# The first chunk's MLP operand made transposed in PSUM, and its opening written out in program order

## The chip, the cores and the metric

The kernel runs on one core of a Trainium2 chip. The metric is the device time of one execution in microseconds. The kernel before took 1027.79, 1029.85 and 1028.12 us in three runs; the median is 1028.12 us.

## The reference

All data is float32. B = 8 batches, H = 8 heads, S = 576 positions, head size D = 64, so a token has 512 features.

```python
scores = where(mask[h], (q @ k.T) / sqrt(D), -1e9)   # heads 0-3: the last 32 positions
attn   = softmax(scores)                             # heads 4-7: every 4th of the last 128
x      = concat_heads(attn @ v)                      # (B, S, 512)
u      = x + ((x.T @ U) @ V).T                       # U: 576x32, V: 32x576, over positions
out    = u + relu(u @ w1) @ w2                       # w1: 512x2048, w2: 2048x512
```

## The kernel before, in words

**The MLP.** The 4608 tokens are 36 tiles of 128 rows. Three tiles make a chunk of 384 tokens; there are 12 chunks. In a chunk the 2048 hidden features are worked through in 16 slices of 128 (index f). `layer1(f)` (L822) is twelve matmuls of 128x384 on TensorE (PE): each float32 operand is split into a high and a low part, and the products high·high (`w1h`·`uth`), low·high (`w1l`·`uth`) and high·low (`w1h`·`utl`) are summed for four blocks of 128 features (index k). ScalarE (ACT) then makes `hh`, the relu rounded to the high part (L833), VectorE (DVE) makes the rest `hl` (L834), and `layer2(f)` (L838) is nine matmuls into three accumulators. On PE the order is layer1(0), layer1(1), layer2(0), layer1(2), layer2(1) and so on.

**The weights** arrive during chunk 0 as raw 64-bit words, two pieces for a slice (`w1` and `w2` of it), after three small pieces (0: `ut`, 1: `vt`, 2: `uv`). So piece 3+2f is the w1 of slice f and piece 4+2f its w2; a buffer `v_7` holds piece 7, the w1 of slice 2. A piece passes through `narrowed` (two ACT operations, L189 and L190), `add_low` (a shift on DVE, L194, and an add on DVE or GpSimd (POOL), L196) and `finish` (the high part by a cast, on ACT at L200 or on DVE at L202, then the low part by a subtract on POOL, L203). `weight_step` (L265) finishes piece i-3, adds piece i-2, narrows piece i-1 and sends for later pieces, and counts i up.

**The opening, batch 0's attention.** Nine groups of four units. For a group g: its k comes by DMA and is spread on POOL (`spread_q`, L306), `score` (L397) puts scores in PSUM, `soften` runs on DVE (L416) and ACT (the exponential, L420), `turn_pe` transposes on PE (L431), ACT copies the result to SBUF as `pt`, `product` multiplies by v on PE (L454), and `place` (a sum, a reciprocal and one or two multiplies on DVE, L460 to L484) writes x. Plain groups write rows of x directly; dilated groups write `xp`, whose rows are permuted, and DMAs (`x<-xp`) bring them to x's order. Then `t_first` (L520) multiplies by U, `t_evict` splits the result `ts`, `mix` (L556) multiplies by V and adds to x on DVE (L558), and `transp` transposes u on PE (L587) and splits it into `uth` (ACT, L592) and `utl` (DVE, L593), which layer1 of chunk 0 reads.

**Order.** `first_batch` (L637) is issued in program order on PE, DVE, ACT and SP; after it a scheduler orders the instructions by priority. Before the first slice five weight steps are issued, then four after each slice of chunk 0, with a late priority, so that the scheduler may place them. Work for batch 1 and later stands in `queue` at positions counted in chunks and is taken out at `slot()` (L816), which is called six times in a slice. PSUM is one pool: in the opening the scores use the accumulators' three buffers, the transposes the two of `ph`, and the products `pv` three of their own.

Of the kernel before, what the change touches and what calls it, by code (L numbers as in the profile page):

```python
# [138 lines left out]
def attention_moe_kernel(ctx: ExitStack, tc: tile.TileContext, qk0, qk1, qk2, vv, masks, wide, ident, ut, vt, uv, w1, w2, out):  # L139
# [88 lines left out]
    def finish_w(f, layer, n):  # L228
        def go(v):
# [3 lines left out]
            narrow_c(v, h, l, nc.vector if n % L_ON_DVE == 0 else nc.gpsimd, n % 4 < H_ON_ACT)  # L233
# [31 lines left out]
    def weight_step():  # L265
        i = at.get(0, NSMALL)
# [6 lines left out]
        if NSMALL <= i - 2 < NPIECE and i - 2 not in added:  # L273
            add_low(i - 2, nc.vector)
# [182 lines left out]
    def place(g, pv):  # L457
# [29 lines left out]
        for t, to, n, r in sorted(moves):  # L487
# [473 lines left out]
```

## Time and profile before

| | before |
|---|---|
| median of the runs | 1028.12 us |
| the profiled execution's own time | 1031.81 us |
| its span in the trace | 1029.3 us |
| mean granted PE clock | 0.978 |
| first matmul of layer1(0) | 53.17 us |
| last matmul of layer1(15) in chunk 0 starts | 167.07 us |
| first matmul of chunk 1 | 179.68 us |
| PE busy / DVE / ACT / POOL | 988.1 / 593.6 / 387.4 / 306.7 us |

The profile is of one execution. Its own time is 2.5 us above its span, which is what lies ahead of the first and behind the last instruction, and 3.7 us above the median of the runs. A row of the timeline has the start in us, the busy time in us, engine, line, operation, output<-inputs, shapes and a count of instructions drawn together; brackets tell the idle time ahead and what ended it. A row of the stage table has a stretch, its length, and for PE, weight loads, DVE, ACT and POOL the busy us (and the instructions), then the granted clock, the share of the DMA engines and GB/s. A row of a group has the count, the summed busy us, the mean ns, the idle time ahead and what ended it.

### The profile page before, as it was taken

The numbers are of one execution on the slowest core, as the hardware profiler recorded it, in microseconds if no ns is written. First come the engines' busy times: TensorE is split into PE (matmuls) and PEld (weight loads), VectorE is DVE, ScalarE is ACT, GpSimd is POOL, SyncE is SP. The second block draws the span as 40 slices with busy tenths as digits, with TensorE's granted clock in tenths as the row PEclk, the third lists the DMA queues.
The fourth block names the chain that finished last, engine by engine and source line by source line (L and its number), as shares of the span: only waits on it lengthen the run. The fifth ranks groups of instructions, "written<-read, shape, count | busy, mean of one in ns | idle before, by whom it ended". The sixth has DMA issues, their size and how long they took to land.

```text
span 1029.3 us, 17998 instructions
## 1 busy us (share of the span) xinstructions
PE 988.1 (96%) x5904; PEld 864.9 (84%) x5904; DVE 593.6 (58%) x1972; ACT 387.4 (38%) x946; POOL 306.7 (30%) x519
## 2 busy tenths in 40 slices
PE   7589986999999999999999999999999999999998
PEld 6378865988888888888898888988888888899997
DVE  3489667676446863766556773666646865311211
ACT  5477445344233441434323541434323442111110
POOL 3266315345022630425222540325313440000000
PEclk9879997899999999999999999999999999999999
DMA  9558445343223422333233422334223421400000
GB/s 248 168 185 283 139 126 153 84 125 103 74 68 96 136 77 72 115 100 110 66 85 96 131 82 70 110 105 113 84 69 100 127 56 31 117 1 1 31 1 31
DMA packets 96764, 102.06 MB, mean 99 GB/s; under 512 B 12801, under 2 KB 83393, under 8 KB 96673
## 3 DMA queue, kind: packets, MB, share of 16 engines
q1 hardware_dynamic: 96672, 100.93, 34.2%
q8 instruction: 47, 0.77, 0.3%
q14 instruction: 45, 0.36, 0.1%
HBM read 78.86 MB, written 17.30 MB: 93 GB/s over the span
## 4 chain that ended last, share of the span: by engine, by line
PE 85%; DVE 2%; DMA 1%; ACT 1%; issue 0%; POOL 0%; DVEq 0%; SPq 0%; ACTq 0%
PE acc L845 38%; PE ph L828 37%; PE pv L454 4%; PE s L384 3%; PE t L534 2%; PE m L556 1%; PE s L397 1%; DMA raw<-w 1%; DVE v L196 1%; DMA zd<-z 0%; DVE v L194 0%; DVE x L870 0%; ACT v L189 0%; DVE z L566 0%; DVE x L558 0%
## 5 line engine op out<-in xcount | busy, mean ns | idle before, releaser
L845 PE MATMUL acc<-w2h,hh 128*128 128x512 f32 x576 | 230.1, 401 | 6.9 <-ACT hh L833 6.9
L845 PE MATMUL acc<-w2l,hh 128*128 128x512 f32 x576 | 230.1, 400 | 0.0
L834 DVE SCALAR_TENSOR_TENSOR hl<-ph,hh 128x384 fp32r<-128x384 f32 x192 | 106.2, 553 | 189.9 <-ACT hh L833 189.2
L845 PE MATMUL acc<-w2h,hl 128*128 128x512 f32 x576 | 211.1, 398 | 1.4 <-DVE hl L834 1.4
L361 POOL TENSOR_TENSOR qks<-qkr,qks 128x160 fp32r<-128x160 f32 x192 | 103.0, 536 | 361.9 <-ACT qks L360 260.1
L833 ACT ACTIVATE hh<-ph 128x384 fp32r<-128x384 f32 x192 | 93.3, 486 | 268.7 <-PE ph L828 257.6
L828 PE MATMUL ph<-utl,w1h 128*128 128x384 f32 x768 | 176.6, 343 | 0.0
L828 PE MATMUL ph<-uth,w1h 128*128 128x384 f32 x768 | 172.7, 343 | 3.2 <-DVE w1h L202 1.6
L828 PE MATMUL ph<-uth,w1l 128*128 128x384 f32 x768 | 173.6, 342 | 0.7 <-POOL w1l L203 0.7
L420 ACT ACTIVATE p<-p,nmax 128x160 f32<-128x160 f32 (+1 forms) x288 | 109.8, 406 | 133.8 <-DVE nmax L416 132.4
L828 PEld LDWEIGHTS ph<-uth,w1h 128*128 128x128 f32 x768 | 139.5, 191 | 20.4 <-DVE w1h L202 1.8
L443 DVE STREAM_TRANSPOSE pt<-p 32x128 f32<-32x128 f32 x432 | 130.1, 301 | 18.7 <-ACT p L420 13.4
L828 PEld LDWEIGHTS ph<-uth,w1l 128*128 128x128 f32 x768 | 138.0, 191 | 1.8 <-POOL w1l L203 1.0
L828 PEld LDWEIGHTS ph<-utl,w1h 128*128 128x128 f32 x768 | 137.5, 191 | 1.7 <-issue 0.2
L845 PEld LDWEIGHTS acc<-w2h,hh 128*128 128x128 f32 x576 | 108.8, 189 | 24.7 <-ACT hh L833 8.2
L845 PEld LDWEIGHTS acc<-w2h,hl 128*128 128x128 f32 x576 | 107.9, 188 | 25.3 <-DVE hl L834 2.6
L845 PEld LDWEIGHTS acc<-w2l,hh 128*128 128x128 f32 x576 | 109.3, 190 | 16.7
L360 ACT CAST qks<-qkr 128x288 fp32r<-128x288 f32 x192 | 81.1, 430 | 96.0 <-PE s L384 56.1
L413 DVE TENSOR_TENSOR p<-s,wide_sb 128x160 f32<-128x160 f32 x192 | 60.0, 320 | 71.2 <-PE s L384 69.4
L364 POOL TENSOR_TENSOR qks<-qkr,qks 64x128 fp32r<-64x128 f32 x192 | 90.5, 471 | 15.1
L503 POOL TENSOR_TENSOR xhl<-x,xhl 128x256 fp32r<-128x256 f32 (+1 forms) x65 | 47.2, 736 | 92.8 <-ACT xhl L501 85.1
L416 DVE CUSTOM_DVE_ANT_0 p<-s,p 128x160 f32<-128x160 f32 x192 | 60.0, 321 | 4.1
(71 smaller groups left out, 864.1 us busy)
## 6 DMA issues: line engine op xcount, KB each, us to landing
qkr<-qk SPq DMA_DIRECT2D x192, 144.0 KB, 2.2
raw<-w SPq DMA_DIRECT2D x26, 512.0 KB, 5.5
v<-vv SPq DMA_DIRECT2D x126, 97.5 KB, 2.2
out<-x SPq DMA_DIRECT2D x36, 256.0 KB, 2.4
zd<-z SPq DMA_DIRECT2D x120, 64.0 KB, 2.1
xt<-zd SPq DMA_DIRECT2D x30, 256.0 KB, 2.8
qkr<-qk SPq DMA_DIRECT2D x18, 224.0 KB, 4.1
x<-xp SPq DMA_DIRECT2D x96, 32.0 KB, 1.9
```

What stands on the lines that cost most here:

```text
L360: nc.scalar.copy(out=t[:, 0:QK2], in_=raw)
L361: nc.gpsimd.tensor_tensor(out=t[:, QK2:], in0=raw[:, P:], in1=t[:, P:QK2].bitcast(F32), op=ALU.subtract)
L364: eng.tensor_tensor(out=t[lo, 0:P], in0=raw[lo, 0:P], in1=t[lo, 0:P].bitcast(F32), op=ALU.subtract)
L413: nc.vector.tensor_tensor(out=p_sb[:, u, :], in0=sp[:, 0:KW], in1=wide_sb[:, kind], op=ALU.add)
L416: nc.vector.tensor_tensor_reduce(out=p_sb[rs, u, 0:w], in0=a, in1=c, scale=-1.0 / 8.0, scalar=3.0e38, op0=ALU.add, op1=ALU.min, accum_out= ...
L420: nc.scalar.activation(out=p_sb[:, u, 0:w], in_=p_sb[:, u, 0:w], func=AF.Exp, bias=nmax[:, u:u + 1], scale=-1.0,)
L443: nc.vector.transpose(out=pt[WIN * k:WIN * (k + 1), :, rs], in_=p_sb[rs, :, o:o + WIN])
L503: eng.tensor_tensor(out=xl[rs], in0=x[rs], in1=xh[rs].bitcast(F32), op=ALU.subtract)
L828: nc.tensor.matmul(ph, lhsT=w[:, k, :], rhs=u[:, k, :], start=(n == 0), stop=(n == len(seq) - 1))
L833: nc.scalar.activation(out=hh, in_=ph, func=AF.Relu)
L834: nc.vector.scalar_tensor_tensor(out=hl, in0=ph, scalar=0.0, in1=hh.bitcast(F32), op0=ALU.max, op1=ALU.subtract)
L845: nc.tensor.matmul(acc[i], lhsT=h[:, ss], rhs=w, start=(f == 0 and n == 0), stop=(f == FC - 1 and n == 2))
```

## The change

Line numbers of the kernel after are higher by 7 to 90: scores are L404, soften L423, the transposes L438, products L461, place L467 to L491, layer1 L907, hh L912, hl L913, layer2 L924, the shift L202, the add L204, the casts L208 and L210, the subtract L211.

**PSUM in the opening.** A pool of its own: two buffers for scores `s`, one for the transposes `ptp`, one for the products `pv`, one for `t`, three for the new operand `u`. It is closed before the MLP.

**The operand of chunk 0** is made transposed in PSUM. For each block of 128 features k, unit products (x as the weights, the identity as the moving operand) put the transposed x in a bank: `turn_plain`, three products of 128 columns for the plain heads (k = 0, 1), and `turn_dilated`, five products of 96, 96, 96, 80 and 16 columns straight from `xp`, with strided output columns, for the dilated heads (k = 2, 3). `mix_turned` adds the mix by one product of 384 columns into the same bank. `split_u` casts it into `uth` (ACT) and subtracts into `utl` (DVE). Mix, add, transposes and splits by tile ahead of layer1(0) are gone.

```python
+    def turn_dilated(k):
+        first_u(k)
+        first = True
+        ds = slice((k - KC // 2) * P, (k - KC // 2 + 1) * P)
+        for p in range(NDP):
+            rows = min(P, S - P * p)
+            for r in range(DIL):
+                lo, hi = max(P * p, RES * r), min(P * p + rows, RES * r + CTOK // DIL)
+                if lo < hi:
+                    o = r + DIL * (lo - RES * r)
+                    nc.tensor.matmul(u_ps[k][:, o:o + DIL * (hi - lo - 1) + 1:DIL], lhsT=xps[p][0:rows, ds],
+                                     rhs=id_sb[0:rows, lo - P * p:hi - P * p], start=first, stop=False)
+                    first = False
+    def mix_turned(k):
+        c, j = divmod(k, KC // 2)
+        nc.tensor.matmul(u_ps[k], lhsT=t_sb[0, c][:, j * P:(j + 1) * P], rhs=vs[:, V0:V1], start=False, stop=True)
```

**x itself** is needed only where chunk 0 ends (its residual). The dilated rows now leave to DRAM (`leave`, 8 DMAs) and come back (`come`, 5 DMAs) at positions in chunk 0, and the mix of batch 0 stands in the queue too. So do the steps on the small piece 2 (`uv`) and the splitting of U.

```python
-        for t, to, n, r in sorted(moves):
+        for t, to, n, r in sorted(moves) if b > 0 else ():
+    queue += [(0.15 + 0.01 * p, lambda p=p: leave(p)) for p in range(NDP)]
+    queue += [(0.22 + 0.005 * i, lambda i=i: come(i)) for i in range(n0)]
+    queue += [(0.18 + 0.012 * i, lambda i=i: mix(0, i, 0)) for i in range(n0)]
+    queue += [(0.27 + 0.008 * i, lambda i=i: mix(0, i, 1)) for i in range(n0)]
+    queue += [(0.04, fetch_rest), (0.10, lambda: narrowed(2)), (0.12, lambda: add_low(2, nc.gpsimd)),
+              (0.14, lambda: finish(2)), (0.17, split_first_u)]
```

**Loads.** The k of a group is sent one group ahead of v, the mask is bf16 (half the bytes), `ut` is sent after v3 and `vt` before v6.

**Order.** Program order holds on PE, DVE, ACT, POOL and SP from the start to the end of chunk 0. The weight steps are one ahead of layer1(0), one after each layer1(f) and one after each layer2(f-1). The high part of w1 is cast on ACT (for f > 0), that of w2 on DVE; the add is on DVE for w1 and on POOL for w2. Layer1(0) takes the blocks k in the order 2, 3, 0, 1.

```python
-            narrow_c(v, h, l, nc.vector if n % L_ON_DVE == 0 else nc.gpsimd, n % 4 < H_ON_ACT)
+            narrow_c(v, h, l, nc.gpsimd, layer == 0 and f > 0)
-            add_low(i - 2, nc.vector)
+            add_low(i - 2, nc.gpsimd if (i - NSMALL) % 2 else nc.vector)
...
+            if c == 0 and f == 0:
+                weight_step()
             layer1(f)
...
+            if c == 0:
+                weight_step()
             if f > 0:
                 layer2(f - 1)
...
-            for _ in range(W_RATE if c == 0 else 0):
+            if c == 0:
                 weight_step()
```

What the change moves, at three places. First PE in the opening, from group 3's scores to group 1's products: `s3` are the scores of group 3, `ptp2` the transposes of group 2, `pv1` the products of group 1, and the brackets name what is waited for. Before:

```order
L397 MATMUL s3_226<-k3_114,q_sb_91 128x96 [waits DMAHW0_49,DVE_49,Pool_49]
L397 MATMUL s3_226<-k3_114,q_sb_91 128x96 x3
L431 MATMUL ptp2_231<-id_sb_70,p2_192 96x128 [waits PE_49,Activation_49]
L431 MATMUL ptp2_231<-id_sb_70,p2_192 96x128 [waits Activation_49] x3
L454 MATMUL pv1_236<-v1_108,pt1_74 64x65 [waits DMAHW5_49,Activation_49]
L454 MATMUL pv1_236<-v1_108,pt1_74 64x65 x7
```

After, the same six rows:

```order
L404 MATMUL s3_238<-k3_114,q_sb_93 128x96 [waits DMAHW7_49,DVE_49,Pool_49]
L404 MATMUL s3_238<-k3_114,q_sb_93 128x96 x3
L438 MATMUL ptp2_243<-id_sb_72,p2_204 96x128 [waits Activation_49]
L438 MATMUL ptp2_243<-id_sb_72,p2_204 96x128 x3
L461 MATMUL pv1_248<-v1_112,pt1_76 64x65 [waits DMAHW6_49,DVE_49,PE_49]
L461 MATMUL pv1_248<-v1_112,pt1_76 64x65 x7
```

The order of the instructions is the same; the products of group 1 now wait for DVE, where `place(0)` frees the one buffer of `pv`, and no longer only for the copied `pt` and v.

Second, DVE in chunk 0 around the `hl` of slice 2 (`hl0_2`), with the shifts, adds and casts of weight pieces (`v_7` is the w1 of slice 2, `v_8` its w2). Before:

```order
L194 TENSOR_SCALAR v_11_985<-v_11_985 128x512
L196 ISA v_11_985<-raw11_746,v_11_985 128x1024
L194 TENSOR_SCALAR v_12_994<-v_12_994 128x512
L202 CAST w1h_0_78<-v_11_985 128x4x128
L558 TENSOR_TENSOR x4_309<-x4_309,m0_4_0_627 64x256
L196 ISA v_12_994<-raw12_755,v_12_994 128x1024
L194 TENSOR_SCALAR v_13_1003<-v_13_1003 128x512
L834 SCALAR_TENSOR_TENSOR hl0_2_1077<-ph0_2_1017,hh0_2_1076 128x384
```

After, the rows that end with `hl0_2` (`p10` is the soften of batch 1's group 10, of which one of four units is shown):

```order
L913 SCALAR_TENSOR_TENSOR hl0_1_647<-ph0_1_631,hh0_1_646 128x384
L210 CAST w2h_0_82<-v_6_617 128x512
L202 TENSOR_SCALAR v_7_626<-v_7_626 128x512
L204 ISA v_7_626<-raw7_156,v_7_626 128x1024
L423 ISA p10_669,nmax10_670<-s10_671,mask_71 128x96
...
L444 COPY pt1_76<-ptp9_688 96x512
L202 TENSOR_SCALAR v_8_654<-v_8_654 128x512
L913 SCALAR_TENSOR_TENSOR hl0_2_723<-ph0_2_706,hh0_2_722 128x384
```

Ahead of slice 2's `hl`, before has handled pieces 11 to 13, the weights of slices 4 and 5; after has handled pieces 7 and 8, the weights of slice 2 itself.

Third, POOL at the same place, with the subtracts that end a piece (`w1l_0`, `w2l_0`: low parts of the slices 0 to 5) and the adds. Before:

```order
L203 TENSOR_TENSOR w2l_0_81<-v_6_636,w2h_0_80 128x512
L203 TENSOR_TENSOR w1l_0_79<-v_7_725,w1h_0_78 128x4x128
L203 TENSOR_TENSOR w2l_0_81<-v_8_734,w2h_0_80 128x512
L203 TENSOR_TENSOR w1l_0_79<-v_9_743,w1h_0_78 128x4x128
L203 TENSOR_TENSOR w2l_0_81<-v_10_752,w2h_0_80 128x512
```

After:

```order
L204 TENSOR_TENSOR v_6_617<-v_6_617,raw6_150 128x512
L211 TENSOR_TENSOR w2l_0_83<-v_6_617,w2h_0_82 128x512
L211 TENSOR_TENSOR w1l_0_81<-v_7_626,w1h_0_80 128x4x128
L204 TENSOR_TENSOR v_8_654<-v_8_654,raw8_620 128x512
L211 TENSOR_TENSOR w2l_0_83<-v_8_654,w2h_0_82 128x512
```

POOL has an add of a w2 piece between the subtracts of each slice, and takes all of them in program order.

More of the change, by code (lines that the diff above doesn't have):

```diff
@@ L558, in mix, with first_u, turn_plain, split_u @@
         nc.vector.tensor_tensor(out=x, in0=x, in1=mp[rs], op=ALU.add)
-    uts = {}
+    u_ps = {}
+    def first_u(k):
+        tag = "s" if len(u_ps) == 3 else "u"
+        u_ps[k] = psum.tile([P, CTOK], F32, tag=tag, name=f"u{k}", bufs=2 if tag == "s" else 3)
+    def turn_dilated(k):
[11 more added lines that the diff above has]
+                    first = False
+    def turn_plain(k, t):
+        if k not in u_ps:
+            first_u(k)
+        nc.tensor.matmul(u_ps[k][:, t * P:(t + 1) * P], lhsT=x_tile(t)[:, k * P:(k + 1) * P], rhs=id_sb,
+                         start=t == 0, stop=False)
+    def mix_turned(k):
+        c, j = divmod(k, KC // 2)
+        nc.tensor.matmul(u_ps[k], lhsT=t_sb[0, c][:, j * P:(j + 1) * P], rhs=vs[:, V0:V1], start=False, stop=True)
+    def split_u(k, part):
+        h, l = (e[:, k, :] for e in uts[0])
+        if part == 0:
+            nc.scalar.copy(out=h, in_=u_ps[k])
+        else:
+            nc.vector.tensor_tensor(out=l, in0=u_ps[k], in1=h.bitcast(F32), op=ALU.subtract)
     turned_x = {}
@@ L705, in first_batch @@
[L705 to L712 removed]
+        mix_turned(2)
+        mix_turned(3)
+        t_first(3, 0)
+        split_u(2, 0)
+        split_u(3, 0)
+        split_u(2, 1)
+        t_evict(0, 0)
+        finish(w0)
+        split_u(3, 1)
+        for k in (0, 1):
+            mix_turned(k)
@@ new lines, in first_batch, with leave @@
+        for k in (0, 1):
+            split_u(k, 0)
+        for k in (0, 1):
+            split_u(k, 1)
+        narrowed(w1)
+        add_low(w1, nc.gpsimd)
+    spare = {}
+    def leave(p):
+        if not spare:
+            spare[0] = dram.tile([S, HALF_D], F32, tag="spare", name="spare", bufs=1)
+        rows = min(P, S - P * p)
+        for r in range(DIL):
+            lo, hi = max(P * p, RES * r), min(P * p + rows, RES * (r + 1))
+            if lo < hi:
+                o = r + DIL * (lo - RES * r)
+                nc.sync.dma_start(out=spare[0][o:o + DIL * (hi - lo - 1) + 1:DIL],
+                                  in_=xps[p][lo - P * p:hi - P * p])
@@ L714, in batch_items, with come @@
+    def come(i):
+        t, row, n, tok = batch_parts(0)[i]
+        nc.sync.dma_start(out=x_tile(t)[row:row + n, HALF_D:], in_=spare[0][tok:tok + n])
     def batch_items(b):
@@ L825, in layer1 @@
             w1h, w1l = held_w[f][0:2]
-            seq = [(w, u, k) for w, u in ((w1h, uh), (w1l, uh), (w1h, ul)) for k in range(KC)]
+            ks = (2, 3, 0, 1) if c == f == 0 else range(KC)
+            seq = [(w, u, k) for w, u in ((w1h, uh), (w1l, uh), (w1h, ul)) for k in ks]
             for n, (w, u, k) in enumerate(seq):
@@ L866, in attention_moe_kernel @@
         layer2(FC - 1)
+        if c == 0:
+            order.__exit__(None, None, None)
         for i in range(CT):
```

220 lines of the change are left out of this document (111 added, 109 removed).

## The prediction

> **What bounds the kernel now.** I read the busy time by stage first: the opening, chunk 0's layers, the change to chunk 1, and the rest.
>
> ```profile
> 0.00:53.20 53.20, 34.30 (x291) 25.72 (x291) 20.97 (x117) 26.00 (x67) 16.67 (x33) 0.89 0.71 201
> 53.20:171.20 118.00, 104.15 (x623) 87.42 (x624) 92.86 (x226) 72.97 (x170) 56.85 (x48) 0.90 0.57 178
> 171.20:185.00 13.80, 9.86 (x36) 8.43 (x36) 10.73 (x36) 6.04 (x15) 5.86 (x12) 0.64 0.64 180
> 185.00:1029.30 844.30, 839.84 (x4959) 743.37 (x4957) 469.08 (x1596) 282.39 (x695) 227.30 (x426) 1.00 0.29 80
> ```
>
> From 185 us on PE is idle for 4.5 of 844 us at full clock: nothing that happens earlier can shorten that stretch, only move it. So the change is worth what it moves the start of chunk 1 by. Ahead of that there are 53 us of opening, in which PE works 34, and 118 us of layers in which it works 104. Next come the ends of these stretches on PE's timeline.
>
> ```profile
> 53.17 1.65 PE L828 MATMUL ph<-uth,w1h 128*128 128x384 f32 x4 [0.68 <-ACT uth L592]
> 167.07 0.86 PE L828 MATMUL ph<-utl,w1h 128*128 128x384 f32 x4
> 179.68 1.48 PE L828 MATMUL ph<-uth,w1h 128*128 128x384 f32 x4
> ```
>
> Layer1(0) starts at 53.17, layer1(15) ends at 167.07 + 0.86 = 167.9, chunk 1 starts at 179.68. The first row's 1.65 us for four products against 0.86 is the half clock. Chunk 1 also begins at half clock, up to about 185: that loses half of 5.3 us, 2.6 us. So before is level with a chunk 1 that starts at full clock at 182.3.
>
> **The opening.** It is the attention of batch 0, group by group. In before PE runs through groups 3 to 6 without a stop:
>
> ```profile
> 14.87 1.13 PE L397 MATMUL s<-k,q_sb 128*128 128x96 f32 x8
> 19.10 1.13 PE L397 MATMUL s<-k,q_sb 128*128 128x96 f32 x8
> 20.60 0.69 PE L454 MATMUL pv<-v,pt 96*64 96x65 f32 x16
> 21.21 1.13 PE L397 MATMUL s<-k,q_sb 128*128 128x96 f32 x8
> 29.10 1.13 PE L397 MATMUL s<-k,q_sb 128*128 128x96 f32 x8
> ```
>
> A group takes 21.21 - 19.10 = 2.11 us. These rows are the scores of groups 3, 5, 6 and 8, and group 3's products.
>
> Gain of the loads. The first groups wait for k:
>
> ```profile
> 7.74 0.85 POOL L309 COPY q_sb<-k 64x256 f32<-64x256 f32 x2 [2.92 <-DMA k<-qk]
> k<-qk SPq DMA_DIRECT2D x9, 320.0 KB, 8.0
> v<-vv SPq DMA_DIRECT2D x9, 195.0 KB, 8.0
> mask<-masks SPq DMA_DIRECT2D x1, 240.0 KB, 3.3
> ```
>
> Up to the end of k1, before moves 320 + 240 + 195 + 64 (the identity) + 320 KB; after moves 320 + 120 + 320. At the 201 GB/s of the opening the 379 KB less are 1.9 us. Group 3's scores then stand at 14.87 - 1.9 = 13.0.
>
> Loss by the one buffer of pv. The products of group g-2 now wait until place(g-3) has read the buffer, and on DVE place(g-3) stands behind the soften of group g, which waits for the scores of g. So PE stands between scores and products in each group, with everything behind it on its queue: the scores of g+1 as well. The links, from group 5:
>
> ```profile
> 20.37 0.26 DVE L416 CUSTOM_DVE_ANT_0 p<-s,mask 128x96 f32<-128x96 f32 x1 [0.57 <-PE ptp L431]
> 21.09 0.16 DVE L460 TENSOR_SCALAR ssum<-pv 128x4 f32<-128x4 f32 x1
> 21.49 0.42 DVE L484 TENSOR_TENSOR xp<-pv,ssum 128x256 f32<-128x256 f32 x1
> ```
>
> Scores to first soften 20.37 - 19.10 = 1.27; four softens 21.09 - 20.37 = 0.72; place 21.49 + 0.42 - 21.09 = 0.82; a hop, taken as 0.06; products 21.21 - 20.60 = 0.61. Sum 3.48 a group instead of 2.11. From group 3 to group 8 that is five periods, 17.4, plus a second multiply in one place (0.42), plus the first two t products that now stand ahead of group 8's scores: 13.0 + 17.4 + 0.4 + 1.0 = 31.8 for the scores of group 8, against 29.10 before.
>
> The end of the opening. The t products cost at most 0.48 each:
>
> ```profile
> L520 PE MATMUL t<-x,u 128*32 128x256 f32 x8 | 2.3, 388 | 0.4 <-DVE x L484 0.4
> ```
>
> From 31.8, one more period of 3.5 to the products of group 6 (35.3) and four t products (1.6; pipelined). Then PE's own queue: two products of a group (0.61 each), one group's transposes (0.5), five t products (0.4 to 0.48), two sets of five unit products, six plain unit products, two mixes ahead of the second t evict. No row shows a unit product with a strided output. Bounds: 0.14 each, by eight score products in 1.13, and 0.48, by a t product; I take 0.25, since columns are 96 rather than 256. They sum to 2.5 and 1.6 to 2.0. In all about 10 us to 45.4; the last t evict (a cast and a subtract) and the last two mixes bring 47.2, and layer1(0) starts at 47.3. Before: 53.17. So the opening gains 5.9 even with the new wait, since mix, add, transpose and split by tile (nine links between PE, DVE and ACT) are gone. Layer1(0) needs w1l of slice 0 (POOL, 48.7), then eight products: its end, E(0), is 50.3.
>
> **Chunk 0.** Here I expect the loss. In before weight pieces are prepared two to four slices ahead. After, w2 of slice f is finished behind hl(f), then w1 of slice f+1 is added on DVE, cast on ACT, subtracted on POOL, and layer1(f+1) needs the result at once: no slice's lead is left. The rows of the links:
>
> ```profile
> L833 ACT ACTIVATE hh<-ph 128x384 fp32r<-128x384 f32 x18 | 8.6, 479 | 3.6 <-PE ph L828 3.6
> L834 DVE SCALAR_TENSOR_TENSOR hl<-ph,hh 128x384 fp32r<-128x384 f32 x18 | 9.9, 551 | 6.3 <-ACT hh L833 6.3
> L200 ACT CAST w1h<-v 128x512 fp32r<-128x512 f32 x8 | 4.9, 607 | 0.1
> L203 POOL TENSOR_TENSOR w1l<-v,w1h 128x512 fp32r<-128x512 f32 x16 | 22.9, 1436 | 34.2 <-ACT w1h L200 19.9 <-ACT v L189 8.4 <-DMA v<-vv 3.0
> ```
>
> and from the middle of chunk 0, a DVE add alone, and one beside a subtract on POOL:
>
> ```profile
> 95.39 0.69 DVE L196 CUSTOM_DVE_ANT_0 v<-raw,v 128x1024 uint16<-128x1024 uint16 x1
> 99.83 0.41 DVE L202 CAST w1h<-v 128x512 fp32r<-128x512 f32 x1
> 100.16 0.42 DVE L194 TENSOR_SCALAR v<-v 128x512 int32<-128x512 int32 x1
> 100.70 1.58 DVE L196 CUSTOM_DVE_ANT_0 v<-raw,v 128x1024 uint16<-128x1024 uint16 x1
> 100.32 1.41 POOL L203 TENSOR_TENSOR w1l<-v,w1h 128x512 fp32r<-128x512 f32 x1 [1.43 <-DVE w1h L202]
> ```
>
> The add beside POOL's subtract takes 1.58 instead of 0.69 and ends 0.55 behind it (102.28 against 101.73): the two do not run together here. After has just this pair in each slice: the cast of w2h starts POOL's w2l, and DVE's add of w1 comes 0.42 later.
>
> So from the end of layer1(f) to that of layer1(f+1): hh 0.48, hl 0.55, w2h 0.41, w2l 1.41, rest of the add 0.55, w1h 0.60, w1l 1.41, eight products 1.6 (two rows of 0.86 less their overlap), hops 0.2: 7.2 us. PE's own work, layer2(f-1) and layer1 and what else comes, hides inside.
>
> Then the queue's work, which program order now puts between these links; its prices:
>
> ```profile
> L437 DVE COPY pt<-ptp 96x512 f32<-96x512 f32 x9 | 6.1, 677 | 0.0
> L420 ACT ACTIVATE p<-p,nmax 128x96 f32<-128x96 f32 x72 | 21.6, 364 | 19.2 <-DVE nmax L416 19.2
> L503 POOL TENSOR_TENSOR xhl<-x,xhl 128x256 fp32r<-128x256 f32 (+1 forms) x65 | 47.2, 736 | 92.8 <-ACT xhl L501 85.1
> ```
>
> Four exponentials take 1.1 to 1.5, a copy 0.68, a soften 0.72, a place 0.82, a POOL split 0.74, a subtract of piece uv up to 1.4. Counted off the order: slices 1, 2, 5 and 10 have one or two of these between the links (1.1, 1.4, 1.5, 1.5), slice 3 the uv piece with a soften and a place (4.8), slice 4 a place, soften, copy and mix ahead of the w2h cast (4.7), slices 6, 7 and 8 soften, place and POOL splits (2.9, 2.6, 4.5), the six others 0.1 to 0.5 (1.5 together). Sum 26.5; the ends are 0 (all of it falls into waits) and 26.5; I take all of it, since the order leaves an engine nothing else to run.
>
> 15 x 7.2 + 26.5 = 134.5, so layer1(15) ends at 50.3 + 134.5 = 184.8. From there before needs 179.7 - 167.9 = 11.8 to chunk 1, partly at half clock; after needs layer2(14), three transposes and layer2(15), 7.1. Chunk 1 starts at 191.9: 191.9 - 182.3 = +9.6.
>
> **The clock.** In before, these stretches stand beside each other:
>
> ```profile
> 24.90:28.30 3.40, 1.78 (x22) 1.12 (x22) 2.32 (x13) 0.98 (x3) 2.64 (x4) 1.00 1.05 357
> 144.50:147.90 3.40, 1.65 (x9) 1.32 (x8) 3.22 (x8) 2.61 (x7) 1.26 (x1) 0.98 0.41 130
> 147.90:151.10 3.20, 3.20 (x22) 2.24 (x21) 1.49 (x6) 0.00 (x0) 0.00 (x0) 0.50 0.14 34
> ```
>
> After a stretch with PE busy 1.65 of 3.40 us, in gaps of no more than 1.75 us, the next 3.2 us ran at 0.50, though PE was busy throughout. With 1.78 of 3.40 the clock stayed. After has about 5 to 6 us of PE work in slices of 7.2 to 12, so a few of the long slices fall under half. Each costs nothing where PE waits anyway, and up to 3 us in the eight products and layer2; bounds 0 and 7, I take +3.4. The Trainium skill, in "TensorE: Matmul & The Clock Gate", section "Why this matters for your kernels", asks only that no idle gap exceed about 3 us, and puts the fall after a whole window of idle. By it the gaps of after cost no clock, and the sum would be 1037.7; the trace has a fall with gaps of 1.75 us, so I keep the term.
>
> **Sum.** +9.6 + 3.4 = +13.0. The profiled execution's span of 1029.3 becomes 1042.3 and its own time of 1031.81 becomes 1044.8; that execution lies 3.7 above the median, and 1028.1 + 13.0 = 1041.1.
>
> **The rivals.**
>
> *Chunk 0 gets faster.* If DVE's add gets in ahead of POOL's subtract, a slice takes 0.48 + 0.55 + 0.41 + 0.42 + 0.69 + 0.60 + 1.41 + 1.6 + 0.2 = 6.36, and if half of the queue's work hides, 13.2 remain: layer1(15) ends at 50.3 + 95.4 + 13.2 = 158.9, chunk 1 starts at 166.0, and no half clock counts: -16.3, about 1011.5 (1003 to 1025 with the unit products, the clock and what hides). For it: PE has only 104 us of work in the 118, and DVE loses adds to POOL. Against it: the pair of rows at 100 us. The sign turns where the fifteen periods reach 124.9 in all (182.3 - 7.1 - 50.3), 8.3 each with what the queue adds.
>
> *The weights come late.* All that moves in chunk 0's first nine slices shares one queue:
>
> ```profile
> raw<-w SPq DMA_DIRECT2D x26, 512.0 KB, 5.5
> ```
>
> A piece takes 5.5 us to land, the spare copy moves 0.59 MB (576 rows of 256 floats) out and back where before moved it once, and SP, in program order, holds the next piece behind `come`, which waits for `leave`. If each of nine slices waits 1.1 more: +10, 1051. Against it: a piece is sent a slice or more ahead.
>
> *The opening does not shorten.* Groups at 3.48 us leave PE about 60% busy; at half clock its own queue of 10 us doubles in part, and layer1(0) starts at 53 again: +6, 1047.
>
> *No change:* gain and loss cancel, 1028.
>
> **How the numbers follow.** About 2 us (0.2%) is what a measurement tells from no change. The forecast, 1041 (own range 1032 to 1050, by the queue's work and the clock), 0.41; chunk 0 faster, 0.38; late weights 0.10; no gain in the opening 0.07; no change 0.04. Slower 0.58, same 0.04, faster 0.38. The range 1010 to 1052 leaves out a quarter of the faster case and half of the late weights' cases, some 0.15.
>
> **What would show it.** In the trace after: scores of groups 4 to 7 about 3.5 us apart, PE released by DVE; layer1(0) at 47; DVE's adds in chunk 0 near 1.5 us; idle time of `ph<-uth,w1l` ended by POOL's `w1l`, some 1 to 3 us a slice; chunk 1 near 192. The prediction is wrong if layer1(15) ends before 175, if those products wait for ACT or the DMA instead, or if the first slices take longer than the later ones by more than the queue's items.

## The result and the profile after

The kernel after takes 1067.18 us (median of 4 runs, 1066.73 to 1069.18) against 1028.44 us of before: ratio 1.0379, interval 1.0361 to 1.0397. The forecast was 1041 us, with a range of 1010 to 1052. The change is slower, as forecast, but by 38.7 us, three times the 13.0 of the forecast.

The stages of after, cut where its own layer1(0) and chunk 1 begin (length, then PE, weight loads, DVE, ACT and POOL busy, granted clock, DMA share, GB/s):

```profile
0.00:49.40 49.40, 33.33 (x308) 26.27 (x308) 19.56 (x113) 22.82 (x62) 15.23 (x32) 1.00 0.63 183
49.40:205.00 155.60, 114.59 (x598) 93.58 (x598) 84.11 (x224) 69.54 (x163) 67.00 (x59) 0.85 0.49 151
205.00:225.00 20.00, 17.98 (x100) 15.63 (x101) 13.99 (x48) 9.65 (x24) 14.09 (x25) 0.91 0.38 116
225.00:1064.00 839.00, 834.92 (x4924) 739.55 (x4922) 466.28 (x1584) 279.79 (x689) 224.96 (x422) 1.00 0.29 81
```

The last stage is as full as before: 4.1 us of idle time in 839. The opening is 3.7 us shorter. The loss is all in chunk 0, where PE works 115 of 156 us, at a mean granted clock of 0.85. PE's timeline of after, the three rows that answer to those of before:

```profile
49.46 0.96 PE L907 MATMUL ph<-uth,w1h 128*128 128x384 f32 x4 [1.45 <-DVE utl L603]
...
209.63 1.45 PE L907 MATMUL ph<-utl,w1h 128*128 128x384 f32 x4
...
217.38 0.86 PE L907 MATMUL ph<-uth,w1h 128*128 128x384 f32 x4
```

Layer1(0) starts at 49.46 (before 53.17), layer1(15) ends at 211.1 (167.9), chunk 1 starts at 217.38, at full clock. By the forecast's own reckoning before is level with a start at 182.3, so +35.1; the spans differ by 1064.6 - 1029.3 = 35.3. The start of chunk 1 carries the whole result, as the forecast said.

**The opening**, PE's rows from group 4's scores to group 5's, and one set of unit products:

```profile
16.76 1.13 PE L404 MATMUL s<-k,q_sb 128*128 128x96 f32 x8
...
19.68 0.69 PE L461 MATMUL pv<-v,pt 96*64 96x65 f32 x16 [1.35 <-issue]
20.30 1.13 PE L404 MATMUL s<-k,q_sb 128*128 128x96 f32 x8
...
40.73 1.44 PE L584 MATMUL u<-id_sb,xp 128*128 128x96 f32 x10
```

A group takes 3.54 us (before 2.11); 1.35 of it is PE's wait ahead of `pv`. The view names no releaser there ("issue"); the run with two buffers, below, shows that it is the one buffer. The last row is one set of five unit products. In these rows a product of plain float32 operands counts twice: the four score products of a group, which the order of the instructions lists as one and three, are x8 here. So a unit product costs 1.44 / 5, some 0.28 us.

**One slice of chunk 0**, slice 7, in the rows of four engines, put in order of time:

```profile
121.49 0.49 ACT L912 ACTIVATE hh<-ph 128x384 fp32r<-128x384 f32 x1 [3.17 <-PE ph L907]
122.01 0.56 DVE L913 SCALAR_TENSOR_TENSOR hl<-ph,hh 128x384 fp32r<-128x384 f32 x1 [5.12 <-ACT hh L912]
122.49 0.42 DVE L210 CAST w2h<-v 128x512 fp32r<-128x512 f32 x1
122.98 1.38 POOL L211 TENSOR_TENSOR w2l<-v,w2h 128x512 fp32r<-128x512 f32 x1 [3.17 <-DVE w2h L210]
123.28 1.64 DVE L204 CUSTOM_DVE_ANT_0 v<-raw,v 128x1024 uint16<-128x1024 uint16 x1
124.84 0.15 DVE L467 TENSOR_SCALAR ssum<-pv 128x4 f32<-128x4 f32 x1
126.12 0.26 DVE L423 CUSTOM_DVE_ANT_0 p<-s,mask 128x96 f32<-128x96 f32 x1
126.49 1.17 ACT L427 ACTIVATE p<-p,nmax 128x96 f32<-128x96 f32 x4 [3.38 <-DVE nmax L423]
127.56 0.60 ACT L208 CAST w1h<-v 128x512 fp32r<-128x512 f32 x1
128.22 1.03 PE L907 MATMUL ph<-uth,w1h 128*128 128x384 f32 x4 [2.17 <-ACT w1h L208]
128.24 1.29 POOL L211 TENSOR_TENSOR w1l<-v,w1h 128x512 fp32r<-128x512 f32 x1 [3.88 <-ACT w1h L208]
129.59 1.65 PE L907 MATMUL ph<-uth,w1l 128*128 128x384 f32 x4 [0.34 <-POOL w1l L211]
131.03 1.48 PE L907 MATMUL ph<-utl,w1h 128*128 128x384 f32 x4
```

It is the forecast's chain, link by link: hh, hl, w2h, w2l, the add that ends 0.56 behind it (124.92 against 124.36), then the queue's place, soften and exponentials, w1h, w1l, eight products. It reaches from 121.4 to 132.5. Every engine waits in it, and the last two rows show what was priced too low: the eight products run at half clock, 2.9 us (129.59 to 132.51) instead of 1.6. The groups of after up to 215 us say the same for all slices:

```profile
L907 PE MATMUL ph<-uth,w1l 128*128 128x384 f32 x64 | 22.0, 485 | 5.6 <-POOL w1l L211 5.6
L907 PE MATMUL ph<-utl,w1h 128*128 128x384 f32 x64 | 20.5, 463 | 0.0
L204 DVE CUSTOM_DVE_ANT_0 v<-raw,v 128x1024 uint16<-128x1024 uint16 x12 | 19.9, 1661 | 0.4
L907 PE MATMUL ph<-uth,w1h 128*128 128x384 f32 x64 | 16.9, 390 | 32.0 <-ACT w1h L208 30.5 <-DVE utl L603 1.4
```

PE waits 30.5 us for `w1h`, in 14 places, and 5.6 for `w1l`, in 13; in before, up to 190 us, its whole wait for both was 3.1 (1.6 and 0.8 for w1h, 0.7 for w1l).

### The profile page after: what moved, and what is told of

Its sections match the earlier page's. It is cut to its first block, busy times and chain, and to the rows that moved or that the text cites. A ratio compares the mean times of both kernels' runs of the same rounds, so it can differ in the third digit from the quotient of the medians.

```text
span 1064.6 us, 18031 instructions
## 1 busy us (share of the span) xinstructions
PE 1000.8 (94%) x5928; PEld 875.0 (82%) x5928; DVE 583.9 (55%) x1965; ACT 381.8 (36%) x937; POOL 321.3 (30%) x537
## 4 chain that ended last, share of the span: by engine, by line
PE 86%; issue 4%; DVE 3%; DMA 2%; POOL 2%; SPq 1%; ACT 1%; DVEq 0%; POOLq 0%; ACTq 0%
PE ph L907 38%; PE acc L924 36%; PE pv L461 4%; PE s L391 3%; PE s L404 2%; PE t L540 2%; POOL w1l L211 1%; DVE v L204 1%; PE m L564 1%; DMA raw<-w 1%; SPq L495 1%; PE ptp L438 1%; DMA spare<-xp 1%; ACT hh L912 1%; DMA k<-qk 0%
## 5 line engine op out<-in xcount | busy, mean ns | idle before, releaser
L913 DVE SCALAR_TENSOR_TENSOR hl<-ph,hh 128x384 fp32r<-128x384 f32 x192 | 106.3, 554 | 233.0 <-ACT hh L912 232.1
L924 PE MATMUL acc<-w2h,hh 128*128 128x512 f32 x576 | 230.8, 401 | 0.0
L924 PE MATMUL acc<-w2l,hh 128*128 128x512 f32 x576 | 229.6, 399 | 0.0
L924 PE MATMUL acc<-w2h,hl 128*128 128x512 f32 x576 | 213.7, 398 | 0.0
L907 PE MATMUL ph<-uth,w1h 128*128 128x384 f32 x768 | 172.5, 343 | 32.0 <-ACT w1h L208 30.5
L912 ACT ACTIVATE hh<-ph 128x384 fp32r<-128x384 f32 x192 | 93.5, 487 | 298.1 <-PE ph L907 286.9
L907 PE MATMUL ph<-uth,w1l 128*128 128x384 f32 x768 | 178.2, 350 | 5.6 <-POOL w1l L211 5.6
L907 PE MATMUL ph<-utl,w1h 128*128 128x384 f32 x768 | 181.1, 350 | 0.0
L907 PEld LDWEIGHTS ph<-uth,w1h 128*128 128x128 f32 x768 | 137.6, 190 | 51.9 <-ACT w1h L208 35.8
L907 PEld LDWEIGHTS ph<-uth,w1l 128*128 128x128 f32 x768 | 140.0, 195 | 10.3 <-POOL w1l L211 10.0
L907 PEld LDWEIGHTS ph<-utl,w1h 128*128 128x128 f32 x768 | 141.5, 197 | 1.7 <-issue 0.2
L924 PEld LDWEIGHTS acc<-w2h,hl 128*128 128x128 f32 x576 | 108.7, 189 | 23.7
L924 PEld LDWEIGHTS acc<-w2h,hh 128*128 128x128 f32 x576 | 109.6, 190 | 16.3 <-issue 0.4
L924 PEld LDWEIGHTS acc<-w2l,hh 128*128 128x128 f32 x576 | 109.2, 190 | 16.1
L461 PEld LDWEIGHTS pv<-v,pt 96*64 96x64 f32 x1152 | 42.1, 142 | 30.1 <-issue 17.1
```

Of the source, the lines that this page charges most:

```text
L461: nc.tensor.matmul(pv[rs, u, :], lhsT=pt[:, u, rs], rhs=loaded[g, 1, i][:, u, :], start=True, stop=True)
L907: nc.tensor.matmul(ph, lhsT=w[:, k, :], rhs=u[:, k, :], start=(n == 0), stop=(n == len(seq) - 1))
L912: nc.scalar.activation(out=hh, in_=ph, func=AF.Relu)
L913: nc.vector.scalar_tensor_tensor(out=hl, in0=ph, scalar=0.0, in1=hh.bitcast(F32), op0=ALU.max, op1=ALU.subtract)
L924: nc.tensor.matmul(acc[i], lhsT=h[:, ss], rhs=w, start=(f == 0 and n == 0), stop=(f == FC - 1 and n == 2))
```

## The experiments

Theory A: the weights have no lead, so the chain above stands between one layer1 and the next. Rivals: B, the weights can't be made faster; C, the queue's items in program order are the loss, whatever the lead; and the half clock and SP's queue as causes of their own. Times are medians; those of one run are marked (1), and the run of before beside them was 1027.9 to 1028.9.

**One weight step more ahead of layer1(0)** (`e1_lead`).

```diff
             if c == 0 and f == 0:
                 weight_step()
+                weight_step()
```

> One weight step more ahead of layer1(0), nothing else: in each slice w1 of slice f+1 is added on DVE before the end of layer1(f) and only its cast and subtract stand behind it. Theory A (no lead: the chain hh, hl, w2h, w2l, add, w1h, w1l stands between one layer1 and the next): the chain falls to 0.5 + 0.6 + 1.4 + 1.6 + hops, some 4.5 us, so PE's own 6 to 7.5 us a slice decide; chunk 1 starts near 170 instead of 217, time 1016 to 1026. Rival B (the weights are made as fast as DMA, ACT, DVE and POOL can): no lead helps, 1058 to 1067. Rival C (the waits are the queue's items in program order, whatever the lead): about 1045.

Measured 1037.14 (ratio to before 1.008, interval 1.0062 to 1.0098): one line takes back 30.0 of the 38.7 us. B falls. A's time of 1016 to 1026 was not reached either. The sixteen ends of layer1 tell why (worked out from PE's rows, start and busy time of each slice's last products; us from one to the next). For slices 9 and 11 to 15 the forecast gives only a sum, and its row has the mean:

| slice | 1 | 2 | 3 | 4 | 5 | 6 | 7 | 8 | 9 | 10 | 11 | 12 | 13 | 14 | 15 |
|---|---|---|---|---|---|---|---|---|---|---|---|---|---|---|---|
| forecast without the clock | 8.3 | 8.6 | 12.0 | 11.9 | 8.7 | 10.1 | 9.8 | 11.7 | 7.5 | 8.7 | 7.5 | 7.5 | 7.5 | 7.5 | 7.5 |
| after | 9.6 | 8.5 | 12.1 | 15.6 | 11.5 | 11.3 | 11.0 | 11.5 | 11.7 | 10.1 | 7.4 | 10.2 | 9.2 | 8.3 | 10.2 |
| with the lead | 7.2 | 5.5 | 7.0 | 16.4 | 15.3 | 6.4 | 6.3 | 13.3 | 7.5 | 5.4 | 7.9 | 5.8 | 7.6 | 6.7 | 10.4 |

With the lead, slices take 5.4 to 8 us, near the 6 to 7.5 of PE's own work that A counted on, but for 4, 5, 8 and 15. There other waits stand. In slice 8 PE waits 3.4 us for splits of x (`xhl`), in slice 15 1.4 for `w1h` and 2.8 for batch 1's q and k (`qks`). In slices 4 and 5 it waits for v, three times; two of these rows, and SP's queue ahead of the first:

```profile
84.98 0.68 PE L461 MATMUL pv<-v,pt 96*64 96x65 f32 x14 [1.45 <-DMA v<-vv]
97.54 1.13 PE L461 MATMUL pv<-v,pt 96*64 96x65 f32 x14 [3.43 <-DMA v<-vv]
```

```profile
77.97 3.86 SPq L495 DMA_DIRECT2D x<-xp  x5
81.94 0.52 SPq L332 DMA_DIRECT2D v<-vv  x1
```

v of batch 1 lands late: on SP, in program order, its second half stands behind the DMAs that bring dilated rows to x. These take some 0.6 us of issuing each, and by the code each set follows a `place`.

**No program order in chunk 0** (`e2_noorder`).

```diff
     first_batch()
+    order.__exit__(None, None, None)
     psum_open.close()
...
         layer2(FC - 1)
-        if c == 0:
-            order.__exit__(None, None, None)
```

> Program order ends with the opening; in chunk 0 the scheduler orders the instructions, from the same places in the code. Theory A (the place of the weight steps makes the chain): the scheduler can take a weight instruction ahead of queue items but the steps stand as late as before, so 1050 to 1062. Rival C (the program order of the queue's items on ACT, DVE and POOL is the cause): 1025 to 1040.

1037.94 (1). Nearest to C's number, but it does not support C against A: the scheduler had piece 9, the w1 of slice 3, added ahead of the `hl` of slice 1 (the third add of a w1 on DVE starts at 76.66, this `hl` at 79.83), so it gave the weights a lead of its own. Layer1(0) starts at 64.2, 14.7 us later than in after, and the total is 29.2 us less, so what follows is some 44 us shorter. The opening is longer since ACT waits three times for raw words of a weight piece, 6.67, 4.61 and 4.01 us, with exponentials and copies of the last groups behind them:

```profile
29.64 0.65 ACT L198 ACTIVATE raw<-raw 128x512 int32<-128x512 uint32 x1 [6.67 <-DMA raw<-w]
...
45.81 0.67 ACT L198 ACTIVATE raw<-raw 128x512 int32<-128x512 uint32 x1 [4.01 <-DMA raw<-w]
```

PE waits 5.14 us there for `pt`, and from 40 to 50 us it runs at a granted clock of 0.50 (after: 1.00). Why the words land late was not tried. So without the program order the opening lost 14.7 us here, and what that order as such costs in chunk 0 is not separated from the lead.

**Two buffers for pv** (`e3_pv2`).

```diff
-        pv = psum.tile(..., bufs=1 if g < NGB else 3)
+        pv = psum.tile(..., bufs=2 if g < NGB else 3)
...
-        tag = "s" if len(u_ps) == 3 else "u"
-        u_ps[k] = psum.tile(..., bufs=2 if tag == "s" else 3)
+        tag = "s" if len(u_ps) >= 2 else "u"
+        u_ps[k] = psum.tile(..., bufs=2)
```

> The products pv get two buffers in the opening, u two instead of three (its last two take those of s). All theories of chunk 0: unchanged there. If the wait for place(g-3) costs what the trace shows (five gaps of 1.35 and one of 1.68 us before pv), layer1(0) starts 5 to 7 us earlier and the time is 1060 to 1063. If something else in the opening takes the place of it (k or v landing, DVE): 1064 to 1067.

1060.96 (1.0316, 1.0299 to 1.0333): 6.2 us less. Layer1(0) starts at 42.9 instead of 49.5, and the scores of groups 3 and 4 stand 2.11 us apart again (13.42 and 15.53). The wait for `place` on the one buffer is shown, at the size forecast. With the lead as well (`c1_lead_pv2`, both edits):

> The lead of one weight step and the two buffers of pv together. If the two costs lie one behind the other, they add: 1037.1 - 6.2 = 1031. If the SP queue, which is late with v in the slices 4, 5 and 8 of the run with the lead, is paced from the start of the kernel rather than from layer1(0), the opening's gain is lost there: 1036 to 1038.

1032.16 (1.0048, 1.0031 to 1.0065): 5.0 of the 6.2 us; the two costs nearly add.

**PE kept busy in its waits** (`e4_warm`).

```diff
+            for n in range(10 if c == 0 and f > 0 else 0):
+                nc.tensor.matmul(ph, lhsT=held_w[f - 1][0][:, n % KC, :], rhs=uh[:, n % KC, :], start=True, stop=True)
             for n, (w, u, k) in enumerate(seq):
```

> Ten more products of 384 columns ahead of each layer1(f) of chunk 0 (f > 0), with the weights of slice f-1 and into the same bank, which layer1(f) then overwrites: PE works while it would wait for w1h. If the half clock makes the chain longer (eight products at 0.50 cost 1.5 us more in some 11 of 15 slices): -10 to -18, 1049 to 1057. If the half clock falls only where PE waits anyway: 1067, or up to 1085 where the ten products themselves (1.8 us, 3.6 at half clock) are late.

1060.54 (1), 6.6 less with 150 products more, and short of the 10 to 18 that were expected. Chunk 0's stage in this run:

```profile
52.00:205.00 153.00, 125.64 (x759) 106.58 (x758) 85.95 (x228) 69.77 (x165) 70.63 (x65) 0.96 0.51 156
```

The clock is 0.96 where it was 0.85. Slices 1, 3, 6, 7, 10, 13 and 15 get 0.9 to 1.4 us shorter, about what eight products at half clock cost more, slice 4 2.7; slice 5 gets 4.4 longer, where PE then waits 3.5 us for v. So the half clock is a cost of its own on the chain, shown at 6.6 us in all and about 11 before slice 5 takes some back; A alone does not have it.

**The queue's items out of the chain** (`e5_items`): the step that finishes w1 ahead of layer2(f-1), not behind it.

```diff
             if c == 0:
                 weight_step()
+                weight_step()
             if f > 0:
                 layer2(f - 1)
                 if f < FC - 1:
                     slot()
-            if c == 0:
-                weight_step()
```

> The weight step that finishes w1 of slice f+1 stands directly behind the one after layer1(f), ahead of layer2(f-1): w1h and w1l no longer stand behind the place, soften and exponentials of the queue that come with layer2(f-1). The chain hh, hl, w2h, w2l, add, w1h, w1l stays. If the queue's items in the chain cost what the order counts (some 26 us together, with the half clock they cause more): 1035 to 1048. If the chain itself and the half clock are the whole of it: 1058 to 1067.

1066.1 (1): no gain, but not for the reason that the rival gives. Slices 2, 3, 6 and 7 fall (8.5 to 7.3, 12.1 to 7.2, 11.3 to 7.6, 11.0 to 9.8), so the items did stand in the chain there. Slices 4 and 5 rise to 17.3 and 14.7, with a wait of 3.3 for v, and slice 11 from 7.4 to 10.9. In the late slices the two steps together put the narrowing of a later piece ahead of the cast of w1, and it waits for a buffer that POOL's `w2l` frees:

```profile
191.86 0.44 ACT L197 ACTIVATE v<-raw 128x256 f32<-128x256 f32 x1 [2.75 <-POOL w2l L211]
...
193.16 0.60 ACT L208 CAST w1h<-v 128x512 fp32r<-128x512 f32 x1
```

**The add ahead of the cast of w2h** (`e6_addfirst`).

```diff
         at[0] = i + 1
+        if NSMALL <= i - 2 < NPIECE and i - 2 not in added and (i - NSMALL) % 2 == 0:
+            add_low(i - 2, nc.vector)
...
-            add_low(i - 2, nc.gpsimd if (i - NSMALL) % 2 else nc.vector)
+            add_low(i - 2, nc.gpsimd)
```

> In the step behind layer1(f), DVE's shift and add of w1 (slice f+1) come ahead of the cast of w2h, so that the add no longer runs beside POOL's subtract w2l. If the add held off by POOL is in the chain as forecast (0.9 us a slice, 15 slices): -10 to -16, 1051 to 1057. If POOL, which then takes w2l later and w1l behind it, gives the time back: 1063 to 1070.

1059.46 (1), 7.7 less, between the two. The lock itself is plain; the same add, in this run:

```profile
L204 DVE CUSTOM_DVE_ANT_0 v<-raw,v 128x1024 uint16<-128x1024 uint16 x12 | 8.3, 692 | 0.4
```

0.69 instead of 1.66 us. Its 0.97 us in twelve slices would be 11.6; a third of it does not arrive, and PE's waits for POOL's `w1l`, which comes later here, rise to 1.4, 1.5 and 2.1 us in slices 4, 10 and 15 (from 0.4, 0.5 and 1.1).

**Relief for SP**, on the kernel with lead and two pv buffers (1032.16). `e7_lead_pool` issues leave and come from POOL, `e8_lead_moves` batch 1's x<-xp.

```diff
-                nc.sync.dma_start(out=spare[0]...
+                nc.gpsimd.dma_start(out=spare[0]...
```

```diff
-            nc.sync.dma_start(out=x_tile(t)[...], in_=xp[r:r + n])
+            (nc.gpsimd if b == 1 else nc.sync).dma_start(out=x_tile(t)[...], in_=xp[r:r + n])
```

> As the run with lead and two pv buffers, with the 13 DMAs of leave and come issued from POOL instead of SP. If SP's issuing (0.4 to 0.9 us for each DMA, in program order) is what holds v back in the slices 4, 5 and 8: 8 us of SP's time go, and 5 to 15 us of the total, 1016 to 1026. If POOL then holds its own subtracts behind come, which waits for leave: no change or slower, 1031 to 1045.

> As the run with lead and two pv buffers, with the 24 DMAs that bring batch 1's dilated rows to x (x<-xp, 15 us of SP's issuing) issued from POOL instead of SP. If SP's issuing is the bound of the long slices: 1010 to 1024, more than by leave and come alone. If POOL becomes the bound, or the data is late for another reason (a buffer of v not free): 1031 to 1045.

1025.63 (1) and 1027.11 (1): 6.5 and 5.1 less. The time is within the first's forecast; the second, with more DMAs off SP, gains less than forecast, since w1l then waits on POOL behind them (3.3 us at slice 4). `e11_spare_v4` and `e9_pool_v4` add a fourth buffer of v (`bufs=3` to `bufs=4`), to the first and to both moves together:

> As the run with lead, two pv buffers and leave and come on POOL, with four buffers of v instead of three. If SP's wait for a free buffer of v, in program order, is a part of the late v: -3 to -8, 1018 to 1023. If only the issuing counts: 1025.

> Lead, two pv buffers, leave, come and batch 1's x<-xp all issued from POOL, and four buffers of v instead of three. If SP holds v back by its issuing and by waiting in program order for a free buffer of v: the slices 4 and 5 fall from 18 and 14.5 us to about 9, 1010 to 1018. If the DMAs on POOL cost as much as they save on SP: 1024 to 1030.

1024.08 (1) and 1029.11 (1). With all of them on POOL, PE waits 8.4 us for w1l in slice 4, which takes 23.4. A queue in program order that also computes is no free place for DMAs that wait.

**A whole slice of lead** (`e10_full_lead`): on `e7_lead_pool`, three steps ahead instead of two, AHEAD 1, the mixes and copies earlier, the larger weight tiles opened a slice earlier.

```diff
-AHEAD = 2
+AHEAD = 1
...
-                weight_step()
-                weight_step()
+                for _ in range(3):
+                    weight_step()
```

> As the run with lead, two pv buffers and leave and come on POOL, but with three weight steps ahead of layer1(0) instead of two (a lead of a whole slice), the queue's mix, leave and come some 0.04 to 0.09 chunks earlier, the larger weight tiles opened a slice earlier, and pieces sent one ahead instead of two (the order of the buffers needs that). If the remaining waits for w1h and w1l (about 2 us a slice at slices 1 and 9 to 14) are the missing half slice of lead: -8 to -15, 1011 to 1018. If SP and the queue's items bound the slices, or the later sending makes raw pieces late: 1022 to 1032.

1048.42 (1), inconclusive: its opening took 7.3 us longer (below, under the hardware), and slices 3, 4 and 8 took 14 to 18 us, with waits of up to 3.0 us for v and 1.9 for a split of x. It shows only that the waits for w1h go, but for 0.2 us in slice 1 and 1.4 in slice 15, and that they are not what bounds those slices.

**Batch 0's mixes**, on `e11_spare_v4`: `e12_mix_apart` spreads them over slices 1 to 4, `e14_no_mix` leaves them out, so that batch 0's residual lacks them, and `e13_lead_warm` repeats the filler with six products.

```diff
-    queue += [(0.18 + 0.012 * i, lambda i=i: mix(0, i, 0)) for i in range(n0)]
-    queue += [(0.27 + 0.008 * i, lambda i=i: mix(0, i, 1)) for i in range(n0)]
+    queue += [((0.05, 0.08, 0.11, 0.16, 0.19)[i], lambda i=i: mix(0, i, 0)) for i in range(n0)]
+    queue += [(0.23 + 0.0125 * i, lambda i=i: mix(0, i, 1)) for i in range(n0)]
```

> As the run with lead, two pv buffers, leave and come on POOL and four buffers of v, with batch 0's ten mixes in the queue spread over slices 1 to 4 instead of 3 to 5. If the mixes' ping-pong of PE and DVE (PE waits 1.3 to 1.5 us for x<-x,m at slices 4 and 5) lengthens these slices: 1016 to 1021. If it is the data of batch 1: 1024.

> As the same run, leaving out batch 0's ten mixes into x (its residual then lacks the mix). Upper bound of what the mixes cost: if they hold slices 4 and 5, these fall to 7 to 9 us each and the time to 1010 to 1016; if the data of batch 1 does, 1021 to 1024.

> As the same run, with six products more ahead of each layer1(f) of chunk 0 (f > 0), overwritten by it. With the lead only a few slices fall to the half clock (1, 4, 5, 13 to 15), so if a filler helps it is by 2 to 5 us; six products where PE does not wait cost 1.0 us in some eight slices, 8 us. Expected 1022 to 1031: slower if the clock is no longer the issue.

1031.18 (1), 1027.07 (1), 1027.08 (1). Beside them, the kernel without these edits took 1025.59 (`e15_spare_v4_again`, below; its twelve runs reach from 1024.5 to 1028.2), so only spreading the mixes made a difference, for the worse. The mixes are not alone in holding slices 4 and 5: without them the slices still take 13.3 and 13.5, and PE waits for v:

```profile
85.22 0.45 PE L461 MATMUL pv<-v,pt 96*64 96x65 f32 x2 [2.59 <-DMA v<-vv]
87.04 1.13 PE L461 MATMUL pv<-v,pt 96*64 96x65 f32 x14 [1.37 <-DMA v<-vv]
```

With the lead a filler gains nothing. The mean granted clock from 46 to 170 us rises from 0.89 to 0.97, but slices without a wait pay for the six products (slice 9 takes 8.5 instead of 7.5). What the half clock still costs with the lead is therefore not shown.

**v ahead of the x<-xp DMAs** (`e16_v_ahead`, on `e11_spare_v4`; `e17_v_ahead6` with six buffers of v).

```diff
                 if b > 0 and 0 < s <= NGB:
                     load_v(g - 1, 0)
+                    if b == 1:
+                        load_v(g - 1, 1)
                 if s >= LAG:
                     weighted(g - LAG, held.pop(g - LAG))
-                if b > 0 and 0 < s <= NGB:
+                if b > 1 and 0 < s <= NGB:
                     load_v(g - 1, 1)
```

> The same kernel as the run with lead, two pv buffers, leave and come on POOL and four buffers of v (one look: 1024.1 against 1027.9 of before), timed in five rounds. If the look holds: ratio 0.995 to 0.998, faster than before and than the change by 43 us.

> As the run with lead, two pv buffers, leave and come on POOL and four buffers of v, with the second half of batch 1's v sent ahead of the x<-xp DMAs instead of behind them. If v is late because it stands behind x<-xp on SP: PE's waits for v at slices 3 to 5 (2.3, 0.9 us and what half clock they bring) go, 1017 to 1022. If SP then waits there for a free buffer of v and holds x<-xp and the weights: 1025 to 1032.

> The same with six buffers of v. If the free buffer was what SP waited for: 2 to 6 us under the run with four. If four were enough: the same within 2 us.

1025.59 for the version without the edit (`e15_spare_v4_again`, five rounds: 0.9977, 0.9966 to 0.9987), 1023.93 with it (0.9956, 0.9941 to 0.9971), 1025.89 with six buffers (0.9974, 0.9962 to 0.9985). The intervals of the first two overlap, so the 1.7 us between them are not clear of the noise; 1017 to 1022 had been expected. The waits for v are gone, and others stand in their place. What is next on SP behind the x<-xp DMAs is the q and k of the next group, and PE now waits for that, and for the adds of batch 0's mixes on DVE, on the timelines of PE and of SP's queue:

```profile
68.71 0.69 PE L404 MATMUL s<-qkr 128*128 128x96 f32 x4 [1.79 <-DMA qkr<-qk]
...
78.47 1.13 PE L404 MATMUL s<-qkr 128*128 128x96 f32 x8 [2.36 <-DVE x L566]
...
86.82 0.69 PE L404 MATMUL s<-qkr 128*128 128x96 f32 x4 [1.75 <-DMA qkr<-qk]
```

```profile
62.09 3.76 SPq L495 DMA_DIRECT2D x<-xp  x6
65.94 1.15 SPq L350 DMA_DIRECT2D qkr<-qk  x2
```

So it was the place in SP's queue, not a free buffer, that made v late. The edit moved the wait by one load and laid bare those of the mixes (2.36, and 1.81 at 89.33); that these eat up its gain is likely, but no run leaves both out. This version is 43 us faster than the change and 0.44% faster than before.

## Why the prediction was wrong, step by step

**Right.** That chunk 1's start carries the result, and the sign. The loads: group 3's scores at 13.23 (forecast 13.0). The new wait for the one buffer of pv: 3.54 a group (3.48), group 8's scores at 32.1 (31.8), and its worth by the run with two buffers, 6.2 us. The chain without a lead: its links in slice 7, its lock between DVE and POOL (the add ends 0.56 us behind w2l, and all twelve adds of 128x1024 take 1.64 to 1.68), and its weight: 30 us come back by one line. One sign that was named did not show: `ph<-uth,w1l` was to wait 1 to 3 us a slice for POOL's w1l and waits some 0.4. PE waits one link earlier, for ACT's w1h, 2.2 us in the mean of 14 places. The chain is the same, since w1l follows w1h and the eight products follow w1l.

**Where the 22.1 us went** by which chunk 1 starts later than forecast (+35.1 against +13.0): 2.5 up to the end of layer1(0) (52.8 against 50.3), 23.8 in the fifteen slices (158.3 against 134.5), -0.8 from there to chunk 1 (6.3 against 7.1), and -3.4, since the clock stood in the forecast as a term of its own.

**The end of the opening**, +2.2 us: the forecast had the last mixes at 47.2 (47.39 measured) and let layer1(0) follow at 47.3. Their split, casts on ACT and three subtracts on DVE behind the cast of slice 0's w1h, stands between, 2.07 us:

```profile
47.36 0.43 DVE L210 CAST w1h<-v 128x512 fp32r<-128x512 f32 x1
47.82 1.58 DVE L603 TENSOR_TENSOR utl<-u,uth 128x384 fp32r<-128x384 f32 x3
```

The unit product was taken at 0.25 and costs 0.28. It stands on the path, in PE's queue, which runs without a pause from 34.9 to 46.0; the 10 us that were summed for it are 10.4. The forecast's lower bound of 0.14 was a misreading: the eight records of a group's scores are four products. (A second slip, without effect: the rival of a faster chunk 0 comes to 1011.8, not 1011.5.)

**The clock, "I take +3.4, bounds 0 and 7".** This is the term that failed most. Ten of the fifteen slices show the last four products of layer1 at 1.44 to 1.49 instead of 0.86, and the four before them at 1.33 to 1.65, so some 1.3 us each, 13 in all. The forecast's own row had shown the condition (PE busy for less than half of a stretch, in gaps of at most 1.75 us); it then expected that in a few of the long slices only, and counted nothing where PE waits anyway. In slice 7 PE is busy for 0.85 of the 3.0 us ahead of `w1h`, and it waits just ahead of the eight products that the chain ends with, so the drop falls on these, in most slices. That a product at half clock lengthens the chain is shown by the filler (-6.6 us, the clock back at 0.96); the 13 are counted from rows. The lowered clock follows from the waits: with the lead alone, five of the fifteen slices have their last four products slowed, not ten. In slice 7 the gaps were 2.17 and 0.34, and the products behind the second ran at half clock. The Trainium skill, in "TensorE: Matmul & The Clock Gate", section "Why this matters for your kernels", asks for no idle gap above about 3 us. The trace and the rule differ here, and a sum by the rule leaves out all 13 us.

**The queue's work, "26.5, I take all of it".** Slices 1 to 3, 6 to 8, 10, 11 and 14 came out within some 1.5 us, the half clock included. Slices 4, 5 and 9 did not: 15.6, 11.5 and 11.7 against 11.9, 8.7 and at most 7.7, with some 1.3 of clock in two of them. In slice 4 scores, transposes and products of batch 1 stood within layer1 itself, at half clock; in slice 5 they stood there and v came 0.7 late; slice 9, one of the six priced at 0.5 or less, has a place, a copy and the t evict (a subtract and two casts), which come ahead of w1h on DVE and ACT:

```profile
149.90 0.36 ACT L555 CAST ts<-t 32x256 fp32r<-32x256 f32 x1 [3.95 <-DVE ts L554]
...
150.66 0.62 ACT L208 CAST w1h<-v 128x512 fp32r<-128x512 f32 x1
```

Without the clock these three slices are some 8 us over. With the 13 of the clock that makes 21 of the 23.8 us by which the fifteen slices exceeded 134.5; the rest is not settled. It shows most in slices 12 and 15, each 2.7 over the mean of 7.5 with the clock in it.

**The rivals.** "Chunk 0 gets faster" failed on the row that stood against it: no add of 128x1024 ran ahead of POOL's subtract, unless the code put it there. "The weights come late" named the right queue and the wrong cargo: PE waits for data of attention, not for weights, and in after this was hidden behind the chain (0.7 us in one row). It became a bound, in slices 4 and 5, only when the lead was given back. "The opening does not shorten" was wrong for after, whose groups run at full rate from the fourth on (scores in 1.13 us).

## What to carry to other kernels

When an order is written out by hand, look for each product's last operand and count the slices between the step that makes it and its use: at zero, every queue's work ahead of it becomes a link, and one step moved ahead can be worth more than all else. Where PE waits just ahead of the critical products, price these at the clock that the trace shows behind such waits. And a queue that issues DMAs in program order passes on each wait to all loads behind it: taking one load out of its way moved the wait to the next. Before a price is read from a row with a count, compare that count with the program's: a record need not be a whole product.

## What the runs showed of the hardware

In the run with the whole slice of lead, PE ran from 10 to 34 us at half rate without a pause, though the view grants it a clock of 1.00 there: group 5's scores took 2.02 us where the same instructions take 1.13 in after. In order, the window and the row:

```profile
20.00:25.00 5.00, 5.00 (x41) 4.13 (x41) 2.54 (x22) 2.54 (x9) 0.00 (x0) 1.00 1.09 281
```

```profile
21.64 2.02 PE L404 MATMUL s<-k,q_sb 128*128 128x96 f32 x8
```

The run with leave and come on POOL, whose opening is the same code but for how far weights are sent ahead, has no such stretch. Why the rate stayed low is open, and a granted clock of 1.00 in a window is thus not proof of full rate: the duration of a known product is.
